# Block queries, keys and values laid out in other runs, part A's output stored by SyncE, nine output-weight pairs loaded inside the first step

## The chip, the cores and the metric

One core of a Trainium2 chip runs the whole program. The metric is the device time of one execution in microseconds. Engines are named as in the profile: PE (TensorE matmuls), PEld (its weight loads), DVE (VectorE), ACT (ScalarE), POOL (GpSimd) and SP (SyncE, which here only issues DMAs). DMAs issued by SP appear on DMA queue q1, those issued by ACT on q10, those issued by POOL on q0. All three share the core's 16 DMA engines.

## The reference, cut to what matters

Two independent parts, joined along the last axis. Part A is a long convolution over 2048 rows of 1024 channels, done by FFT. Part B is a recurrent attention over 64 segments of 32 rows: each segment is led by 8 memory rows that the segment before produced.

```
# part A                                     # part B, for s in range(64):
kv  = shift_conv(k, shift_k) * v             h = concat([mem, x[32*s:32*s+32]])   # 8 + 32 rows
y   = irfft(rfft(kv) * rfft(ssm_k))          q, k, v = h @ Wq, h @ Wk, h @ Wv     # 32 heads of 128
out = q * (y + kv * ssm_D)                   p = softmax(mask(q @ k.T / sqrt(128)))
                                             o = (p @ v) @ Wo
                                             mem = o[:8]; outs.append(o[8:])
```

Only the 8 memory rows and the first 24 rows of `x` of a segment feed the next one. The last 8 rows of each segment, called block rows here, depend on no earlier segment as far as their own queries, keys and values go. 64 x 8 = 512 of them are projected in bulk, ahead of the recurrence.

## The kernel before, in words

The program has two phases. Instructions are issued in the order in which the Python code runs; there is no reordering.

**Part A, 0 to about 407 us.** Four stages, one after another: `stage1` on the filter (scratch `SK1` in DRAM) and, from 70 us, on `kv` (`SU1`); from 176 us the products in the frequency domain, 34 half units that load `Kg` and `Ug` from the scratches and store `SZ`; from 298 us the last stage, 16 rounds `t`. In a round of the last stage `load_z(t + 2)` (L636) issues the loads of `zt` (three buffers, L627) and `qt` (three buffers, L629) on SP, PE makes `y_ps` from `zt` (L642), DVE multiplies it by `qt` into `ot` (two buffers, L645), and POOL stores `ot` to the output (L646). Right after the last round SP issues four `park_w` loads (L676).

Between those instructions, `rows.half(n)` puts in pieces of the bulk projection of the block rows: PE multiplies weights by `hTB` into `ps_q`, `ps_k`, `ps_v` (L173, L176), ACT or DVE empties them. Heads go in four groups `g` of eight. For a group, queries and keys of all 64 segments are gathered in the SBUF tile `stq` (16 KB a partition) and stored to the DRAM tensor `QKBd` by one DMA on ACT's queue (L184). Values are gathered in `stv` 128 rows at a time and stored to `VBd` by four DMAs on POOL's queue, one for each pair of heads `c` (L188). Weights that stay in SBUF are loaded by `res_half` (L112, SP, 256 KB each), the others into a ring of eight (L144). POOL also copies 17 weight pairs from the inputs to DRAM tensors `Wst` (`relay`, L121).

```
183              if m == "k" and j == 7:
184                  nc.scalar.dma_start(QKBd[:, :, g, :].rearrange("s e x -> e s x"),
185                                      self.st[:].rearrange("e s h t r -> e s (h t r)"))
186              if m == "v" and j % 2 == 1:
187                  for c in range(4):
188                      nc.gpsimd.dma_start(VBd[16 * rb:16 * rb + 16, c, g],
189                                          self.sv[:, rb, c * 256:(c + 1) * 256])
```

**Part B's recurrence, about 422 to 2107 us.** A loop over 64 segments `s`, in each of it four groups `g` of heads. For a group, `qk_part` (L748) and `v_part` (L763) project the segment's own rows, `tr_a` transposes and puts the block rows' keys beside them (L785, from `qkb`), `scores` (L807 to L822) and `softmax` follow, `pv` (L848, L850) uses the values and the block values `VB`, and `wo` (L865) adds up the output. After the loop PE makes the output of the block rows (L982).

SBUF does not hold all weights. `resident` pairs stay; 17 pairs of 512 KB, `streamed`, are loaded anew in every step through a ring of five tiles `wring`: `place` (L711) issues the next load on SP, and `done` calls it as soon as PE has used a tile. Each step also loads `qkb` (128 KB of QKBd, SP, L791, issued near the end of the step before, one buffer), `VB` (64 KB of VBd, POOL, L801) and the rows `H` (ACT, L660).

Eleven of the output-weight pairs ("o") are resident. Two are loaded at the end of part A. The memory of the other nine is free only once the bulk projection is over; the loop at L902 issues their 18 halves (L112) on SP, after the first five ring tiles and `qkb`, ahead of the first step:

```
898  for _ in range(RING):
899      place()
900  load_vb(0)
901  qkb = load_b(0)
902  for key in resident:
903      if key[0] == "o" and key not in n_o:
904          for n in range(2):
905              res_half(key, n)
```

Of the kernel before, what the change touches and what calls it, by code (L numbers as in the profile page):

```python
# [9 lines left out]
BF = mybir.dt.bfloat16  # L10
# [11 lines left out]
def fused_kernel(ctx: ExitStack, tc, q, k, v, shift_k, ssm_k, ssm_D, outa, x, mem0, Wq, Wk, Wv, Wo, outb, n_seg):  # L22
# [11 lines left out]
    nc = tc.nc  # L34
# [12 lines left out]
    dram = ctx.enter_context(tc.tile_pool(name="b_dram", bufs=1, space=DRAM))  # L47
    SU1 = dram.tile([128, 32, D], BF, name="SU1")
    SK1 = dram.tile([128, 32, D], BF, name="SK1")
    SZ = dram.tile([128, 32, D], BF, name="SZ")  # L50
    QKBd = dram.tile([n_seg, 128, 4, 128], BF, name="QKBd")
    OLd = dram.tile([n_seg, 128, 256], BF, name="OLd")
    VBd = dram.tile([n_seg, 4, 4, 8, 256], BF, name="VBd")

    pairs = [("qk", g, i) if i < 8 else ("v", g, i - 8) for g in range(4) for i in range(12)]
    pairs[-4:-4] = [("o", 0, i) for i in range(4)]
# [3 lines left out]
    resident = [key for key in pairs if key not in streamed and key not in parked]  # L60
# [65 lines left out]
    class Rows:  # L126
# [27 lines left out]
        def half(self, n, by="A"):  # L154

            for _ in range(n):
                if self.at == 192:
                    return
                iu, j, lo = self.at // 16, self.at % 16 // 2, self.at % 2 * 4
                m, g = units[iu]  # L160
                self.load_to(iu * 8 + 8)
                ws = self.loaded[iu * 8:iu * 8 + 8]
                assert len(ws) == 8
                if lo == 0:
                    self.ps = ps_p.tile([128, 512], F32, tag="pp", name="ps_" + m)
                if m == "q" and self.at % 16 == 0:
                    self.st = stq.tile([128, n_seg, 8, 2, 8], BF, tag="stq", name="stq")
                if m == "v" and self.at % 16 == 0:
                    self.sv = stv.tile([128, 4, 1024], BF, tag="stv", name="stv")
                rb, cs = j // 2, slice(j % 2 * 512, j % 2 * 512 + 512)  # L170
                for kc in range(lo, lo + 4):
                    if m == "v":
                        nc.tensor.matmul(self.ps[:], lhsT=hTB[:, kc, rb * 128:(rb + 1) * 128], rhs=ws[kc][:, cs],  # L173
                                         start=(kc == 0), stop=(kc == 7))
                    else:
                        nc.tensor.matmul(self.ps[:], lhsT=ws[kc][:, j * 128:(j + 1) * 128], rhs=hTB[:, kc, :],  # L176
                                         start=(kc == 0), stop=(kc == 7))
                if lo:
                    if m == "v":
                        self.evac(self.sv[:, rb, cs], self.ps[:], by)  # L180
                    else:
                        self.evac(self.st[:, :, j, int(m == "k"), :], self.ps[:].rearrange("e (s r) -> e s r", r=8), by)
                    if m == "k" and j == 7:
                        nc.scalar.dma_start(QKBd[:, :, g, :].rearrange("s e x -> e s x"),  # L184
                                            self.st[:].rearrange("e s h t r -> e s (h t r)"))
                    if m == "v" and j % 2 == 1:
                        for c in range(4):
                            nc.gpsimd.dma_start(VBd[16 * rb:16 * rb + 16, c, g],  # L188
                                                self.sv[:, rb, c * 256:(c + 1) * 256])
                self.at += 1  # L190
                self.load_to(self.at // 16 * 8 + 8 + self.at % 16 // 2 + 4)

# [5 lines left out]
    def rows_view(ap2d, t):  # L198
        return ap2d.rearrange("(p r) d -> r p d", r=16)[t]
# [415 lines left out]
    with ExitStack() as c3:  # L615
        io = c3.enter_context(tc.tile_pool(name="a3_io", bufs=3, side="right"))
        wk = c3.enter_context(tc.tile_pool(name="a3_wk", bufs=2, side="right"))
        ps_big = c3.enter_context(tc.tile_pool(name="a3_ps", bufs=3, space=PSUM))
        open_res(12)
        rows.load_to(rows.at // 16 * 8 + 16)  # L620
        relay(3)
        zts = {}

        def load_z(t):
            if t < 16:
                zt = io.tile([128, 2, 1024], BF, tag="zt", name="zt")
                nc.sync.dma_start(zt[:], SZ.rearrange("m (h r) d -> r m h d", h=2)[t])  # L627
                qt = wk.tile([128, 1024], BF, tag="qt", name="qt", bufs=3)
                nc.sync.dma_start(qt[:], rows_view(q, t))  # L629
                zts[t] = zt, qt  # L630

        load_z(0)
        load_z(1)
        rows.go(4)
        for t in range(16):
            load_z(t + 2)  # L636
            rows.half(2 + t % 2)
            zt, qt = zts[t]
            pt = ps_big.tile([128, 1024], F32, tag="big", name="y_ps")
            for hf in range(2):  # L640
                for h in range(2):
                    nc.tensor.matmul(pt[:, hf * 512:(hf + 1) * 512], lhsT=G2h[h][:, :],  # L642
                                     rhs=zt[:, h, hf * 512:(hf + 1) * 512], start=(h == 0), stop=(h == 1))
            ot = wk.tile([128, 1024], BF, tag="ot", name="ot")
            nc.vector.tensor_tensor(out=ot[:], in0=pt[:], in1=qt[:], op=ALU.mult)  # L645
            nc.gpsimd.dma_start(rows_view(outa, t), ot[:])  # L646
    ca.close()
    open_res(2)
    act = cw_.enter_context(tc.tile_pool(name="b_act", bufs=1))
# [138 lines left out]

    def load_b(s):
        qkb = act.tile([128, 4, 128], BF, tag="qkb", name="qkb")  # L790
        nc.sync.dma_start(qkb[:], QKBd[s])  # L791
        return qkb

    def new_u(g):
        u = G()
        u.g = g
        u.qkb = qkb[:, g, :]
        return u

    def load_vb(s):  # L800
        nc.gpsimd.dma_start(VB[:], VBd[s].rearrange("c g r x -> (c g r) x"))  # L801

    def scores(u):
        S = ps_ts.tile([128, 4, 40], F32, tag="ts", name="S")
# [94 lines left out]
        place()  # L899
    load_vb(0)  # L900
    qkb = load_b(0)
    for key in resident:  # L902
        if key[0] == "o" and key not in n_o:
            for n in range(2):
                res_half(key, n)
    hT = new_hT()
    h_rows(H, hT, 0)
    for s in range(n_seg):
        us = []
        for g in range(4):  # L910
            if g == 2 and s + 1 == n_seg:
                spare = [key for key in resident if key[0] != "o" and key[1] < 2 and key not in early]
                for key, at in zip([key for key in streamed if key[0] == "o"], spare):
                    nc.sync.dma_start(res[at][:], Wst[key][:])
                    res[key] = res[at]
            u = new_u(g)
            us.append(u)
            qk_part(u, range(0, 4))
            unpark()
            if g >= 1:  # L920
                S = scores(us[g - 1])
            if g >= 2:
                pv(us[g - 2], s, (0, 1))
            if g >= 1:
                softmax(us[g - 1], S)
            qk_part(u, range(4, 6))
            if g >= 2:
                pv(us[g - 2], s, (2, 3))
            qk_part(u, range(6, 8))
            qk_out(u)  # L930
            if g < 3:
                v_part(u, range(0, 8))
                tr_a(u)
                v_out(u)
            unpark()
            if g == 3 and s + 1 == n_seg:
                for s0, s1 in ((0, 32), (32, s)):
                    nc.sync.dma_start(OLs[:, s0:s1].rearrange("e s h r -> e s (h r)"),
                                      OLd[s0:s1].rearrange("s e x -> e s x"))
        Y = ps_acc.tile([128, 512], F32, tag="acc", name="yacc")  # L940
        wo(us[0], Y)
        tr_a(us[3])
        v_part(us[3], range(0, 8), Y)
        v_out(us[3])
        if s + 1 < n_seg:
            H = load_h(s + 1)
        S = scores(us[3])
        if s + 1 < n_seg:
            qkb = load_b(s + 1)
        softmax(us[3], S)  # L950
        pv(us[2], s, (0, 1), "aqaq")
        wo(us[1], Y, range(0, 4))
        pv(us[2], s, (2, 3), "aqaq")
        wo(us[1], Y, range(4, 8))
        wo(us[2], Y)
        pv(us[3], s, (0, 1, 2, 3), "aqta")
        wo(us[3], Y)
        if s + 1 < n_seg:
            hT = new_hT()
            h_rows(H, hT, 8)  # L960
        Y_sb = act.tile([128, 256], BF, tag="PT", name="Y_sb")
        nc.scalar.copy(Y_sb[:], Y[:, 256:512])  # L962
        if s + 1 < n_seg:
            fill_mem(hT, Y_sb)
            idle = ps_acc.tile([128, 512], F32, tag="acc", name="idle")
            keep_warm(idle, 2)
        for dq in range(4):
            nc.gpsimd.dma_start(outb[32 * s:32 * s + 24, dq * 256:(dq + 1) * 256], Y_sb[32 * dq + 8:32 * dq + 32, :])  # L968
        if s + 1 < n_seg:
            load_vb(s + 1)  # L970
# [88 lines left out]
```

## Time and profile before

| | |
|---|---|
| three runs | 2161.88, 2166.8, 2180.03 us (median 2166.8) |
| profiled execution | 2169.6 us, span 2167.7 us, mean granted PE clock 0.959 |
| busy share of the span | PE 82%, PEld 48%, DVE 50%, ACT 39%, POOL 19% |
| DMA | 732.15 MB, mean 338 GB/s |
| q1 (SP) | 683.05 MB, 85.2% of 16 engines' span |
| q0 (POOL), q10 (ACT) | 28.88 MB, 4.2%; 14.62 MB, 2.7% |
| ring loads (L711) | 448 of Wstqk, 320 of Wstv, 315 of Wsto, 512 KB each, 5.9 to 6.4 us to landing |

A share is the part of the span in which an engine was busy, averaged over stages that have different limits. A landing time runs from the issue of a DMA to its completion. In lists of groups the time behind "|" is first the busy time and the mean of one instruction, then the idle time of the engine just ahead of it and what ended most of it.

### The profile page before, as it was taken

The numbers are of one execution on the slowest core, as the hardware profiler recorded it, in microseconds if no ns is written. First come the engines' busy times: TensorE is split into PE (matmuls) and PEld (weight loads), VectorE is DVE, ScalarE is ACT, GpSimd is POOL, SyncE is SP. The second block draws the span as 40 slices with busy tenths as digits, with TensorE's granted clock in tenths as the row PEclk, the third lists the DMA queues.
The fourth block names the chain that finished last, engine by engine and source line by source line (L and its number), as shares of the span: only waits on it lengthen the run. The fifth ranks groups of instructions, "written<-read, shape, count | busy, mean of one in ns | idle before, by whom it ended". The sixth has DMA issues, their size and how long they took to land.

```text
span 2167.7 us, 87967 instructions
## 1 busy us (share of the span) xinstructions
PE 1781.4 (82%) x37808; PEld 1048.6 (48%) x37808; DVE 1091.4 (50%) x3235; ACT 835.5 (39%) x2538; POOL 407.9 (19%) x841
## 2 busy tenths in 40 slices
PE   5777977768888888888888888888888888888889
PEld 2332222345555555555555554555555555555558
DVE  6885842244444445455444455555544545444530
ACT  5445741223334334343334333433333434333320
POOL 4013642201111111111111111111111211111110
PEclk8989998989999999999999999999999999989999
DMA  7798979899999999999999999999999999999990
GB/s 259 271 325 276 364 238 335 256 360 363 363 366 348 356 366 377 346 378 372 357 366 370 351 368 357 376 373 353 373 345 367 364 358 357 358 327 361 351 337 21
DMA packets 275652, 732.15 MB, mean 338 GB/s; under 512 B 65679, under 2 KB 85023, under 8 KB 275261
## 3 DMA queue, kind: packets, MB, share of 16 engines
q1 hardware_dynamic: 214414, 683.05, 85.2%
q0 software_dynamic: 18368, 28.88, 4.2%
q10 hardware_dynamic: 42480, 14.62, 2.7%
q8 instruction: 295, 4.83, 0.9%
q14 instruction: 95, 0.78, 0.1%
HBM read 676.14 MB, written 59.18 MB: 339 GB/s over the span
## 4 chain that ended last, share of the span: by engine, by line
PE 46%; DMA 35%; issue 8%; DVE 5%; ACT 4%; POOL 1%; SPq 0%; ACTq 0%; DVEq 0%; POOLq 0%
DMA wring<-Wstv 16%; PE qkacc L748 13%; DMA wring<-Wstqk 9%; PE yacc L865 9%; PE vacc L763 4%; PE otacc L848 3%; PE yacc L763 3%; PE pl L982 3%; PE tp L777 2%; DMA wring<-Wsto 2%; DMA H<-in_B_x_dram 2%; PE ps_v L173 1%; PE ps_k L176 1%; PE otacc L850 1%; PE ps_q L176 1%
## 5 line engine op out<-in xcount | busy, mean ns | idle before, releaser
L748 PE MATMUL qkacc<-Wqk,hT 128*32 128x512 bf16 x4096 | 351.0, 383 | 3.7 <-issue 3.7
L853 ACT CAST OT<-otacc 128x80 bf16<-128x80 f32 x1024 | 183.3, 234 | 391.5 <-PE otacc L850 385.5
L856 POOL COPY OL<-OT 128x64 bf16<-128x64 bf16 x252 | 64.6, 257 | 1328.6 <-ACT OT L853 1328.6
L763 PEld LDWEIGHTS <-hT 128*32 128x32 bf16 x8192 | 213.4, 97 | 174.5 <-issue 107.3
L865 PE MATMUL yacc<-Wo,OT 128*32 128x256 bf16 x5632 | 258.5, 287 | 24.3 <-issue 20.1
L748 PEld LDWEIGHTS <-hT 128*32 128x32 bf16 x8192 | 177.3, 96 | 207.2 <-issue 59.4
L865 PEld LDWEIGHTS <-OT 128*32 128x32 bf16 x8192 | 216.9, 100 | 91.4 <-issue 54.8
L748 PE MATMUL qkacc<-wring,hT 128*32 128x512 bf16 x2048 | 205.9, 388 | 20.7 <-DMA wring<-Wstqk 19.2
L848 PE MATMUL otacc<-PT,vsb 32*128 32x64 bf16 x2048 | 147.3, 193 | 58.9 <-ACT OT L853 48.9
L763 PE MATMUL vacc<-wring,hT 128*32 128x256 bf16 x2560 | 117.2, 276 | 79.2 <-DMA wring<-Wstv 78.1
L786 DVE COPY QT<-tp 128x256 bf16<-128x256 bf16 x256 | 74.7, 292 | 198.4 <-PE tp L777 192.2
L717 ACT COPY wring<-park 128x1024 bf16<-128x1024 bf16 x128 | 129.9, 1015 | 114.5 <-PE qkacc L748 110.0
L748 PE MATMUL qkacc<-Wearly,hT 128*32 128x512 bf16 x2048 | 164.6, 395 | 8.3 <-DVE hT L891 4.3
L821 DVE TENSOR_REDUCE mx<-S 128x4 f32<-128x160 f32 x256 | 83.1, 325 | 170.5 <-PE S L818 167.5
L754 ACT CAST qks<-qkacc 128x512 bf16<-128x512 f32 x256 | 150.5, 588 | 40.6 <-PE qkacc L748 36.9
L832 DVE TENSOR_REDUCE sm<-P 128x4 f32<-128x256 bf16 x256 | 107.6, 420 | 102.9 <-ACT P L830 102.9
L763 PE MATMUL vacc<-Wv,hT 128*32 128x256 bf16 x3584 | 157.7, 274 | 0.3 <-issue 0.2
L865 PE MATMUL yacc<-wring,OT 128*32 128x256 bf16 x2520 | 140.0, 287 | 17.4 <-issue 15.8
L850 PE MATMUL otacc<-PT,VB 32*128 32x64 bf16 x2048 | 143.5, 190 | 8.9 <-issue 7.2
L883 DVE COPY hT<-x_tp 128x192 bf16<-128x192 bf16 (+1 forms) x64 | 23.0, 359 | 236.5 <-PE x_tp L882 236.5
L968 POOL DMA_DIRECT2D out_dram<-Y_sb x256 | 129.7, 513 | 37.7 <-ACT Y_sb L962 34.7
L848 PEld LDWEIGHTS <-vsb 32*128 32x128 bf16 x2048 | 84.5, 93 | 105.5 <-issue 95.9
(220 smaller groups left out, 2926.6 us busy)
## 6 DMA issues: line engine op xcount, KB each, us to landing
wring<-Wstqk SPq DMA_DIRECT2D x448, 512.0 KB, 6.4
wring<-Wstv SPq DMA_DIRECT2D x320, 512.0 KB, 5.9
wring<-Wsto SPq DMA_DIRECT2D x315, 512.0 KB, 6.1
SK<-s_sb SPq DMA_DIRECT2D x8, 1024.0 KB, 6.6
SU<-s_sb SPq DMA_DIRECT2D x8, 1024.0 KB, 7.3
QKBd<-stq ACTq DMA_DIRECT2D x4, 2048.0 KB, 20.5
Kg<-SK SPq DMA_DIRECT2D x16, 512.0 KB, 8.1
Ug<-SU SPq DMA_DIRECT2D x16, 512.0 KB, 8.4
```

Source lines behind the costliest of these rows:

```text
L717: nc.scalar.copy(t[:, 0, :], park[key][0][:])
L748: nc.tensor.matmul(u.qk[p0:p0 + 32, :], lhsT=hT[:, kc, :], rhs=w[t][:, c2 * 512:(c2 + 1) * 512], start=(kc == 0), stop=(kc == 7), tile_pos ...
L754: nc.scalar.copy(u.qks[:], u.qk[:])
L763: nc.tensor.matmul(u.vacc[32 * c:32 * c + 32, 0:256], lhsT=hT[:, kc, :], rhs=w[kc % 2][:, c * 256:(c + 1) * 256], start=(kc == 0 and Y is ...
L786: nc.vector.tensor_copy(u.QT[:].rearrange("e (c j) r -> e c j r", c=2), tv[:, 0])
L821: nc.vector.tensor_reduce(out=mx[:], in_=S[:], op=ALU.max, axis=AX.X)
L832: nc.vector.tensor_reduce(out=sm[:], in_=P[:], op=ALU.add, axis=AX.X)
L848: nc.tensor.matmul(o, lhsT=u.v[r, i * 128:(i + 1) * 128], rhs=PTv[r, i, 0], start=True, stop=False, tile_position=(32 * c, 0))
L850: nc.tensor.matmul(o, lhsT=VB[r, i * 128:(i + 1) * 128], rhs=PTv[r, i, 1], start=False, stop=True, tile_position=(32 * c, 0))
L853: nc.scalar.copy(u.OT[:, 2 * c:2 * c + 2, :], ov[:, :, 0:40])
L865: nc.tensor.matmul(Y[32 * dq:32 * dq + 32, 256:512], lhsT=u.OT[:, hh, 0:32], rhs=w[hh % 2][:, dq * 256:(dq + 1) * 256], start=(u.g == 0 an ...
L968: nc.gpsimd.dma_start(outb[32 * s:32 * s + 24, dq * 256:(dq + 1) * 256], Y_sb[32 * dq + 8:32 * dq + 32, :])
```

## The change

Four edits. `QKBd` is laid out by group: a store writes whole runs of 16 KB per partition, and the load of a segment gathers four pieces of 256 B per partition (before: 1 KB in one piece). `VBd` is laid out by pair of heads, group, segment: one store takes all four pairs of 128 rows, and a load takes 16 runs of 4 KB (before: 64 KB in one run). Part A's output is stored by SP instead of POOL. The 18 halves of the nine output-weight pairs are issued six at a time, ahead of groups 0, 1 and 2 of the first step. The tiles, the arithmetic and the order of the instructions of PE, DVE and ACT are as before.

```
-    QKBd = dram.tile([n_seg, 128, 4, 128], BF, name="QKBd")
+    QKBd = dram.tile([4, 128, n_seg * 128], BF, name="QKBd")
...
-    VBd = dram.tile([n_seg, 4, 4, 8, 256], BF, name="VBd")
+    VBd = dram.tile([4, 4, n_seg, 8, 256], BF, name="VBd")
...
                     if m == "k" and j == 7:
-                        nc.scalar.dma_start(QKBd[:, :, g, :].rearrange("s e x -> e s x"),
-                                            self.st[:].rearrange("e s h t r -> e s (h t r)"))
+                        nc.scalar.dma_start(QKBd[g], self.st[:].rearrange("e s h t r -> e (s h t r)"))
                     if m == "v" and j % 2 == 1:
-                        for c in range(4):
-                            nc.gpsimd.dma_start(VBd[16 * rb:16 * rb + 16, c, g],
-                                                self.sv[:, rb, c * 256:(c + 1) * 256])
+                        nc.gpsimd.dma_start(VBd[:, g, 16 * rb:16 * rb + 16].rearrange("c s r x -> (s r) c x"),
+                                            self.sv[:, rb, :].rearrange("p (c x) -> p c x", c=4))
...
             nc.vector.tensor_tensor(out=ot[:], in0=pt[:], in1=qt[:], op=ALU.mult)
-            nc.gpsimd.dma_start(rows_view(outa, t), ot[:])
+            nc.sync.dma_start(rows_view(outa, t), ot[:])
...
     def load_b(s):
         qkb = act.tile([128, 4, 128], BF, tag="qkb", name="qkb")
-        nc.sync.dma_start(qkb[:], QKBd[s])
+        nc.sync.dma_start(qkb[:], QKBd[:, :, s * 128:(s + 1) * 128].rearrange("g e x -> e g x"))
...
     def load_vb(s):
-        nc.gpsimd.dma_start(VB[:], VBd[s].rearrange("c g r x -> (c g r) x"))
+        nc.gpsimd.dma_start(VB[:], VBd[:, :, s].rearrange("c g r x -> (c g) r x"))
...
     load_vb(0)
     qkb = load_b(0)
-    for key in resident:
-        if key[0] == "o" and key not in n_o:
-            for n in range(2):
-                res_half(key, n)
+    n_o = [key for key in resident if key[0] == "o" and key not in n_o]
...
     for s in range(n_seg):
         for g in range(4):
...
+            for key in (n_o[3 * g:3 * g + 3] if s == 0 else ()):
+                for n in range(2):
+                    res_half(key, n)
             u = new_u(g)
```

## The prediction

> **What bounds the kernel now.** I read the windows by stage first, then the DMA view of single stretches, then the queue's own waits, then the time line around each stall. The windows put the loop over the 64 segments (467 to 2043 us) beside four stretches ahead of it. Columns: PE, PEld, DVE, ACT, POOL busy, granted clock, DMA share, GB/s.
>
> ```profile
> 70.00:176.00 106.00, 86.20 (x370) 36.78 (x367) 88.26 (x129) 52.08 (x71) 8.44 (x16) 0.94 0.81 273
> 176.00:216.00 40.00, 28.52 (x152) 8.70 (x152) 26.92 (x45) 22.12 (x41) 21.07 (x23) 0.91 0.99 306
> 318.00:356.00 38.00, 23.69 (x99) 9.97 (x98) 8.57 (x7) 5.28 (x9) 9.80 (x19) 0.81 0.94 285
> 422.00:431.00 9.00, 5.66 (x122) 2.96 (x126) 2.65 (x8) 2.88 (x4) 1.65 (x3) 1.00 0.63 215
> 467.00:2043.00 1576.00, 1329.81 (x33396) 815.52 (x33400) 791.72 (x2677) 609.67 (x2123) 252.47 (x607) 0.97 0.98 361
> ```
>
> In the loop the 16 DMA engines are busy 98% of the time and PE 84%: the weight tiles streamed into the ring set the step, so DMA time added to a step lengthens it. Ahead of the loop the rate falls to 285 to 306 GB/s while the engines stay 94 to 99% busy: they move something inefficient. The DMA view of 185 to 215 us names it (packets, MB, share):
>
> ```profile
> q1 hardware_dynamic: 2941, 5.56, 51.8%
> q10 hardware_dynamic: 8208, 2.10, 33.0%
> ```
>
> That is one QKBd store on ACT's queue: 2 MB in 8192 packets of 256 B, 33.0% x 16 x 30 us / 8208 = 19.3 ns each. It takes 158 engine-us, 9.9 us of all 16 engines. The page gives the two transfers of this tensor (KB each, median us to landing):
>
> ```profile
> qkb<-QKBd SPq DMA_DIRECT2D x64, 128.0 KB, 6.1
> QKBd<-stq ACTq DMA_DIRECT2D x4, 2048.0 KB, 20.5
> ```
>
> SP waits for that landing: in the program's list of waits the DMAs of SP and ACT take eight completion semaphores in turn, and the eighth DMA after a store waits for it. The queue's own waits (total, times, longest), and PE's stalls in the time line:
>
> ```profile
> SPq L627 <- DMA QKBd<-stq: 18.4, 1, 18.4
> ...
> SPq L112 <- DMA QKBd<-stq: 11.4, 1, 11.4
> SPq L519 <- DMA QKBd<-stq: 9.6, 1, 9.6
> ...
> SPq L112 <- DMA VBd<-stv: 7.3, 1, 7.3
> ```
>
> ```profile
> 216.68 0.64 PE L547 MATMUL Kre_ps<-Kg,Mre 128*64 128x512 bf16 x2 [4.17 <-DMA Kg<-SK]
> ...
> 352.47 1.89 PE L642 MATMUL y_ps<-zt,G2h 128*128 128x512 bf16 x4 [12.08 <-DMA zt<-SZ]
> ...
> 446.52 0.62 PE L763 MATMUL vacc<-wring,hT 128*32 128x256 bf16 x8 [15.03 <-DMA wring<-Wstv]
> ```
>
> The first two stalls follow stores 2 and 3; the last is the first step, where SP has 18 output-weight halves (4.7 MB) ahead of the ring's next tile, and none of them starts before the last VBd store has landed.
>
> **The change, part by part.** The order of PE, DVE and ACT stays the same; POOL loses 16 part A stores and 48 VBd stores, SP gains the 16, and 12 of the 18 halves move behind ring loads.
>
> *QKBd stores as whole runs (4).* Runs of 16 KB replace 8192 pieces. The trace has no such store; the nearest are the 4 KB packets, 174 ns on average in the packet records of the loop, so 2 MB is 512 x 174 = 89 engine-us, 5.6 us of all engines, against 9.9. Bounds: 5.1 (4 KB at the median of 159 ns) and 9.9 (no gain). I take 5.6 and a landing near 8 us. What that is worth, store by store:
> Store 1 (110.9 us): SP stands still until 131.4, an SU store takes 11.2 us, weights issued at 135.7 reach PE at 145.3. PE's last product of the stage starts at 172.1, though DVE ended its input at 166.9, having lost 3.7 us itself to PE. PE cannot pass DVE: at most 3.7 + 5.2 less a normal lag of 1.2 = 7.7. I take 6.5 (3 to 7.7).
> Store 2 (193.1): the stall of 4.2 goes; the half units then run at their cadence of 3.1 us on PE. 4 (0 to 4.2).
> Store 3 (324.8): PE loses 12.1, but the stretch to 386 is held by DMA, so I count DMA time: 4.3 us of packets, and about 4 us in which the engines ran dry while SP was held (342 to 351). 8.5 (3 to 13).
> Store 4 (407.1): SP waits until 420.7 for PE to free ring memory, so this DMA time is spare. 0.
> Sum 19 us (6 to 25).
>
> *Part A's stores on SP.* Sixteen issues of 0.55 us leave POOL, where they hide behind nothing that is late. On SP each waits for DVE's ot (1.22 us each), and behind it queue zt and qt of three rounds later and a weight half. qt already waits for ot(t), since it has three buffers; zt waits for PE's product of the same round, 1.2 us earlier. From an issue, zt needs 7.6 us, y_ps 1.0, ot 1.2: 10 us for three rounds, 3.4 a round, against some 3.7 now, which DMA sets at 396 GB/s. So nothing inside the stage, if the store lands in the 5.7 us it takes now; if it lands like qt behind the loads of its own queue (7.3), two rounds take 0.3 + 7.3 + 1.2 = 8.8 us, 0.7 a round longer, 11 us in all. At the end, park_w was issued at 384.5 ahead of the last ot; it now comes behind it (385.7), and PE already waits 3.4 us for it: +2. I take +2 (0 to +13).
>
> *VBd stores 128 rows at once.* 64 stores of 0.53 us of POOL become 16 with four times the rows each. Bounds for one: 0.53 to 2.1 us; POOL has room either way. In DRAM the pieces stay 512 B. The last one goes out near 422 instead of 425.5, where POOL had also stood 3.2 us, so the Wo halves start some 3 us earlier. The VB load (64 KB, 4.8 us) keeps pieces of 512 B per partition and is used in a later group: 0.
>
> *Wo inside the first step.* The bytes are the same. Six halves instead of 18 stand ahead of the next ring tile, which is issued near 430 instead of 440.5; PE gains about 10 us there, but 3.1 MB (8.5 us) then compete with the ring in the rest of the step. As the loop is held by DMA from the next step on, what stays is the DMA time that no longer runs dry: 0.37 x 9 us = 3.3 in 422 to 431. I take 3.5, with the VBd edit (0 to 10).
>
> *The load of a block, 64 times.* Now 128 packets of 1 KB, 47 ns each in the packet records, 6.0 engine-us. After it, each partition gathers four pieces of 256 B: 512 pieces. The trace has no 256 B read. Its bounds: a quarter of the 1 KB packet, 11.8 ns (no loss), and the piece of 512 B in the OLd load at the end, 2 KB packets of four pieces at 117 ns, 29 ns. The 256 B store piece, 19.3 ns, is nearest. The pieces of a partition lie 128 x 8192 x 2 bytes apart, 2 MiB. 512 x 19.3 = 9.9; (9.9 - 6.0) / 16 = 0.24 us a step, 15.6 us over 64, times 0.98: 15. Where pieces share the engines with other queues they overlap (the shares add up to more than 100% in parts of the stores), so I take 13 (0 to 36). Its latency has cover: issued at 1002.8, first used at 1011.1; 8.3 us against 6.1.
>
> The Trainium skill, "DMA: Bandwidth & Descriptors", section "Latency and other measured facts", speaks against this edit: a row pitch of 2 MiB cuts copies to 164 GB/s from 207 at 512 KiB, and that is the pitch here. By its ratio the piece would cost 24 ns, an estimate from that page, the loss 25 us and the whole change +4.5. No run here has that pitch; it is weighed below.
>
> *Sum.* -19 + 2 - 3.5 + 13 = -7.5 us against the profiled execution: 2169.6, of which the span is 2167.7. Its time is 2.8 above the median of the runs, 2166.8. A run after: 2166.8 - 7 = 2160.
>
> **The rivals.** *The load is free in the loop.* For it: overlapping packets, and 2% of 26 us of DMA idle, in which 0.24 us would fit. Against: the idle is in crumbs, and PE waits 106 times for a Wstv tile alone (78 us). With part A's gain at 24 and the first step's at 3.5: 2166.8 - 27.5 = 2139; with the upper ends of both, 2132.
>
> *The pieces of one load hinder one another,* as they all lie at power-of-two distances and 16 engines read them at once. For it: a gathered 512 B piece (64 KB pitch) takes 29 ns, a single one (H) 27. Against: zt, in 2 KB runs at 32 KB pitch, takes 88 ns a run, as plain runs do. Halfway between 19.3 and 29, 24 ns: (12.3 - 6.0) / 16 x 64 = 25 us, 12 over the forecast's 13: 2172. The rule cited above is of this kind; no trace agrees with it yet.
>
> *The load is dear.* A piece read alone costs well over a piece stored; SP's queue is served in order, so the ring tile behind each of the 64 loads is late by it. At 29 ns: (14.9 - 6.0) / 16 x 64 = 36 us, 2182. At 40 ns, twice the row: 58 us, 2204. It decides from 32 ns on, where the loss passes 42 us and the total 2189. Against: 512 B pieces already cost 29.
>
> *SP's order takes part A's gain back.* The store lands in 7.3 us behind its own queue's loads, +11, and store 3 then gives nothing: 2160 + 11 + 8.5 = 2179.5.
>
> *The 16 KB runs are no faster than the pieces:* the stores keep 20 us, all of the 19 goes, 2179.
>
> **How the numbers follow.** Forecast 2160 at 0.34, own range 2146 to 2176; the free load 0.32; hindered pieces 0.09; the dear load 0.17; SP's order 0.05; no faster stores 0.03. About 1%, 22 us, is what a measurement of this kernel can tell. Faster by more: the free load and a little of the forecast, 0.35. Slower by more: the dear load and some of the last two, 0.19. Within: 0.46. Range 2132 (all upper gains, no loss) to 2190 (a piece at 32 ns).
>
> **What would show it.** Right: no QKBd wait on SP over 3 us, stores landing under 10 us, part A some 18 us shorter (the loop's second step starting near 446 instead of 467), the 15 us stall at L763 under 6, and the loop some 13 us longer, with qkb landing near 7 us and a DMA share still at 0.98. Wrong: a loop that is not longer, one longer by over 30 us, or DVE's wait for out_dram growing past 27 us.

## The result, and the profile after

The changed kernel takes 2161.4 us (median of 13 runs, 2146.3 to 2170.0) against 2170.0 for the kernel before in the same session (13 runs, 2161.9 to 2180.0): ratio 0.995, 95% interval 0.9929 to 0.9971. A second session gave 2158.4 against 2175.2, 0.9928 (0.9898 to 0.9958). Both lie within the 1% named as no change, 9 to 17 us on the faster side; the prediction was 2160, 7 us faster. The profiled execution of after took 2148.3 us (span 2146.4), 13 us less than its own median, so its absolute times flatter the change; I read differences between landmarks, not its span.

The windows of after, over the stretches that answer to those shown of before (same columns: PE, PEld, DVE, ACT, POOL busy, granted clock, DMA share, GB/s). Line numbers of after are two lower from the middle of the file on.

```profile
70.00:168.00 98.00, 83.15 (x363) 36.35 (x369) 88.26 (x129) 52.54 (x71) 3.07 (x4) 0.98 0.83 296
168.00:208.00 40.00, 31.55 (x167) 9.91 (x171) 27.28 (x46) 24.36 (x45) 20.04 (x20) 0.91 1.01 361
304.00:342.00 38.00, 31.29 (x129) 13.04 (x129) 10.45 (x9) 7.04 (x12) 3.08 (x4) 0.91 0.99 357
404.00:412.00 8.00, 4.46 (x84) 2.28 (x84) 1.38 (x4) 2.88 (x4) 1.30 (x2) 1.00 0.71 238
448.00:2024.00 1576.00, 1324.81 (x33419) 809.97 (x33409) 791.59 (x2678) 609.66 (x2125) 249.92 (x604) 0.98 0.99 361
```

The first stretch holds the same DVE work (88.26 us) in 98 us that took 106. In the second and third, the DMA engines are a little busier than before (1.01 and 0.99 against 0.99 and 0.94; a share above 1 comes of packets whose times overlap) and move 361 and 357 GB/s in place of 306 and 285. The fourth, the first step, still has its engines only 71% busy. The DVE, ACT and POOL work of the loop is the same.

The DMA view of 180 to 200 us around store 2 of `QKBd` (packets, MB, share of 16 engines), and the two transfers of this tensor from the DMA view of the whole execution (KB each, median us to landing):

```profile
q1 hardware_dynamic: 2480, 4.67, 69.5%
q10 hardware_dynamic: 144, 2.10, 25.2%
```

```profile
QKBd<-stq ACTq DMA_DIRECT2D x4, 2048.0 KB, 10.9
...
qkb<-QKBd SPq DMA_DIRECT2D x64, 128.0 KB, 6.2
```

The store is now 128 packets of 16 KB (and 16 small ones): 25.2% x 16 x 20 us = 81 engine-us, 5.0 us of all engines in place of 9.9. It lands in 10.9 us where it took 20.5 (medians of 10.2 to 12.0 in all ten traces of the new layout, 16.7 to 20.5 in the four of the old); the load lands in 6.2 where it took 6.1.

SP's own waits, from the list of after in its order (total, times, longest), and PE's stalls in the time line:

```profile
SPq L709 <- PE qkacc L746: 366.3, 370, 4.0
SPq L709 <- DMA wring<-Wstqk: 291.2, 297, 3.7
...
SPq L112 <- DMA VBd<-stv: 7.4, 1, 7.4
...
SPq L644 <- DMA QKBd<-stq: 5.7, 1, 5.7
...
SPq L112 <- DMA QKBd<-stq: 3.4, 1, 3.4
```

```profile
323.04 1.89 PE L640 MATMUL y_ps<-zt,G2h 128*128 128x512 bf16 x4 [5.33 <-DMA zt<-SZ]
...
372.03 1.03 PE L683 MATMUL park_t<-ident,park_w 128*128 128x128 bf16 x8 [6.02 <-DMA park_w<-in_B_Wv_dram]
...
420.59 0.62 PE L761 MATMUL vacc<-wring,hT 128*32 128x256 bf16 x8 [6.56 <-DMA wring<-Wstv]
...
429.01 0.40 PE L761 MATMUL vacc<-wring,hT 128*32 128x256 bf16 x8 [2.61 <-DMA wring<-Wstv]
...
436.89 0.40 PE L863 MATMUL yacc<-wring,OT 128*32 128x256 bf16 x8 [2.37 <-DMA wring<-Wsto]
```

Of 39.4 us in which SP stood for a `QKBd` store, 9.1 are left. The stall after store 2 is gone, that of 12.1 after store 3 has become 5.3, and the 15.0 of the first step 6.6, 2.6 and 2.4. What is left after store 3 is not SP's wait: the `zt` tile that PE stands for there was issued at 310.8, 0.2 us behind the store, and took 12.2 us to land, where the median is 6.9. The wait for park_w grew from 3.4 to 6.0, and the VBd wait stayed. The first two lines bear on the loop: SP stands longest not for transfers but for PE's products at L746, which hand back the ring tile that the next load needs. It was so before the change:

```profile
SPq L711 <- PE qkacc L748: 383.9, 375, 4.0
SPq L711 <- DMA wring<-Wstqk: 260.1, 299, 3.3
```

Landmarks of the time line, us (first Kg load: start of part A's second stage; first zt load: of its last; third ring load: end of part A; H load of the second and the last segment: the loop):

```
                     Kg     zt     ot first..last  3rd ring   H 2nd   H last
before              176.0  307.5   315.5..384.4     420.7     459.1   2069.2
after               167.9  293.8   301.8..363.6     402.4     440.3   2048.6
after, 2nd session  175.0  300.5   309.6..370.9     410.3     448.3   2049.0
```

### The profile page after: what moved, and what is told of

It is laid out like the page before. It is cut to its first block, busy times and chain, and to the rows that moved or that the text cites. A ratio compares the mean times of both kernels' runs of the same rounds, so it can differ in the third digit from the quotient of the medians.

```text
span 2146.4 us, 87846 instructions
## 1 busy us (share of the span) xinstructions
PE 1770.8 (83%) x37779; PEld 1041.6 (49%) x37808; DVE 1091.0 (51%) x3235; ACT 836.3 (39%) x2538; POOL 377.1 (18%) x777
## 4 chain that ended last, share of the span: by engine, by line
PE 47%; DMA 34%; DVE 8%; issue 6%; ACT 5%; POOL 0%; SPq 0%; ACTq 0%; DVEq 0%; POOLq 0%
DMA wring<-Wstqk 13%; PE qkacc L746 12%; DMA wring<-Wstv 12%; PE yacc L863 9%; DMA wring<-Wsto 4%; PE otacc L846 3%; PE vacc L761 3%; PE yacc L761 3%; PE pl L980 3%; PE tp L775 3%; DMA out_dram<-ot 2%; PE ps_k L176 1%; PE ps_v L173 1%; PE otacc L848 1%; DVE S L820 1%
## 5 line engine op out<-in xcount | busy, mean ns | idle before, releaser
L746 PE MATMUL qkacc<-Wqk,hT 128*32 128x512 bf16 x4096 | 350.4, 383 | 3.2 <-issue 3.2
L854 POOL COPY OL<-OT 128x64 bf16<-128x64 bf16 x252 | 64.6, 256 | 1331.7 <-ACT OT L851 1331.7
L746 PEld LDWEIGHTS <-hT 128*32 128x32 bf16 x8192 | 178.3, 96 | 213.2 <-issue 69.8
L863 PE MATMUL yacc<-Wo,OT 128*32 128x256 bf16 x5632 | 252.8, 282 | 27.1 <-issue 22.7
L863 PEld LDWEIGHTS <-OT 128*32 128x32 bf16 x8192 | 212.2, 98 | 96.7 <-issue 63.5
L746 PE MATMUL qkacc<-wring,hT 128*32 128x512 bf16 x2048 | 206.9, 390 | 28.0 <-DMA wring<-Wstqk 26.1
L746 PE MATMUL qkacc<-Wearly,hT 128*32 128x512 bf16 x2048 | 165.3, 398 | 6.9 <-DVE hT L889 3.6
L863 PE MATMUL yacc<-wring,OT 128*32 128x256 bf16 x2520 | 135.3, 280 | 23.0 <-issue 16.1
## 6 DMA issues: line engine op xcount, KB each, us to landing
QKBd<-stq ACTq DMA_DIRECT2D x4, 2048.0 KB, 10.9
```

The costliest lines, as they stand in the source:

```text
L746: nc.tensor.matmul(u.qk[p0:p0 + 32, :], lhsT=hT[:, kc, :], rhs=w[t][:, c2 * 512:(c2 + 1) * 512], start=(kc == 0), stop=(kc == 7), tile_pos ...
L863: nc.tensor.matmul(Y[32 * dq:32 * dq + 32, 256:512], lhsT=u.OT[:, hh, 0:32], rhs=w[hh % 2][:, dq * 256:(dq + 1) * 256], start=(u.g == 0 an ...
```

## The experiments

Every ratio is to the kernel before on the same chip. Its interval is about 0.3% to either side, 6.5 us, so a difference between two kernels is good to about 9 us; where less is read, it is from landmarks in the traces.

Theory, from the prediction: `QKBd`'s stores give part A about 19 us and its gathered loads take 13 back in the loop, with little from the rest. Rivals: the load is free; the load is dear; the gain comes from the other edits.

### The changed kernel once more

> The changed kernel once more, for a second profile and as a base for the others. The prediction's theory (part A and the first step give some 20 us, the gathered load takes some 13 us back in the loop): 0.995 of before, near 2160 us, and in a profile at before's granted clock (0.96) the loop from the second step's qkb issue to the last one near 1620 us against 1610 before. The rival (the load is free, and the first profile's loop of 1608 us is the rule): a loop within 3 us of before whatever the clock, so a time near 2148.

2158.4 us, 0.9928 (0.9898 to 0.9958): the reference for the three that follow, which ran beside it. The loop in its trace, 1600.7 us at a clock of 0.964, is neither the 1620 of the theory nor within 3 us of before's 1610. One execution does not settle it: in the eight traces with the gathered load once a step the loop takes 1600.7 to 1628.3 us (median 1612), and the two loops without a load, which are one program, read 1594.9 and 1601.3.

### QKBd's edit undone

```
-    QKBd = dram.tile([4, 128, n_seg * 128], BF, name="QKBd")
+    QKBd = dram.tile([n_seg, 128, 4, 128], BF, name="QKBd")
...
-                        nc.scalar.dma_start(QKBd[g], self.st[:].rearrange("e s h t r -> e (s h t r)"))
+                        nc.scalar.dma_start(QKBd[:, :, g, :].rearrange("s e x -> e s x"),
+                                            self.st[:].rearrange("e s h t r -> e s (h t r)"))
...
-        nc.sync.dma_start(qkb[:], QKBd[:, :, s * 128:(s + 1) * 128].rearrange("g e x -> e g x"))
+        nc.sync.dma_start(qkb[:], QKBd[s])
```

> The changed kernel with QKBd in its old layout (256 B pieces stored, 1 KB pieces loaded), the other three edits kept. Prediction's theory: the other edits alone give about 1.5 us, so within 4 us of before, ratio 0.998 to 1.001; part A long again (ring loads at L709 near 420 us instead of 402), loop 13 us shorter than with the gathered load. Rival (load free): 18 us over the changed kernel, that is 8 to 10 us slower than before or equal to it with something else lost in the loop.

2174.9 us, 1.0021 (0.9992 to 1.005): nothing is left of the gain. It is 16.5 us over the changed kernel, near the 18 that the rival of a free load named; its loop, 1610.0 us, is not the 13 us shorter than the loops with the gathered load that the theory had. SP's list has the store's waits again:

```profile
SPq L645 <- DMA QKBd<-stq: 12.0, 1, 12.0
SPq L518 <- DMA QKBd<-stq: 11.1, 1, 11.1
...
SPq L112 <- DMA QKBd<-stq: 10.5, 1, 10.5
```

The other three edits together are worth nothing that can be measured.

### The load taken out of the loop, in either layout

The same edit in the new layout and in the old one:

```
-        if s + 1 < n_seg:
-            qkb = load_b(s + 1)
```

> The changed kernel without the 63 loads of qkb inside the loop: every segment uses segment 0's block queries and keys. Beside the changed kernel this prices the gathered load. Prediction's theory: 9.3 engine-us a load (512 pieces at 18.1 ns) is 0.57 us of all 16 engines, so 36 us shorter than the changed kernel if the loop is held by DMA alone, 2125 us. Rival (load hidden): less than 10 us shorter.

> QKBd in its old layout and no load of qkb in the loop (segment 0's block queries and keys for all), the other edits kept. Beside undo_qkbd this prices the load in 1 KB pieces: 6.0 engine-us, 0.38 us, 24 us in all by the prediction's theory; near 0 by the rival. Beside noload_gather, whose loop is the same, it gives part A's share of the layout alone: 19 us by the prediction, some 18 by the two profiles.

With the gathered layout 2146.4 us, 0.9871 (0.9839 to 0.9904); with the whole one 2166.0, 0.997 (0.9941 to 0.9999). Two differences follow. Between the two, without any load in the loop, lies what the stores alone are worth: 19.6 us. Against the kernels with the load, a gathered load costs 2158.4 - 2146.4 = 12.0 us over the loop and a whole one 2174.9 - 2166.0 = 9.0. The gather's surplus is 3 us, where its DMA time is 13; but 3 is a difference of differences, uncertain by some 13.

Neither load's DMA time comes back in full when the load is gone: a gathered one's 9.3 engine-us (512 records of 18.1 ns) are 0.58 us of all engines, 36.6 us over 63 loads, of which 12 came back; of 23.6 for the whole ones, 9 came back, each uncertain by some 9. The window of the loop without the gathered load, and SP's first wait, show how little room there is:

```profile
448.00:2024.00 1576.00, 1330.23 (x33628) 818.44 (x33624) 795.65 (x2688) 614.66 (x2139) 256.08 (x616) 0.98 0.97 359
```

```profile
SPq L709 <- PE qkacc L746: 386.0, 370, 4.0
```

With no load of it at all, DMA still reads 0.97 (0.99 with it) and the rate does not rise. SP's wait for PE at L746 is 386 us here (366 with the loads). I read from this that the loop is not set by DMA alone: its queue waits on PE for free ring tiles and PE waits on it for full ones.

### The load five times

To enlarge the surplus, the load is issued five times a step, four times into tiles that nothing reads; the ring gives up one of its five tiles for the space. A twin does the same in the old layout.

```
-    RING = 5
+    RING = 4
...
             qkb = load_b(s + 1)
+            for i in range(4):
+                xq = xp.tile([128, 4, 128], BF, tag=f"xq{i}", name=f"xq{i}")
+                nc.sync.dma_start(xq[:], QKBd[:, :, (s + 1) * 128:(s + 2) * 128].rearrange("g e x -> e g x"))
```

> The changed kernel, with each step's load of block queries/keys (a 256 B gather) issued five times, the four extra ones into tiles of their own that nothing reads, and the weight ring cut from five tiles to four to make room. It is read against its twin with whole 1 KB pieces. By the packet records a gathered load takes 9.3 engine-us against 6.0 for a whole one, 0.2 us of all engines. Theory 1 (this DMA time is paid in full in a loop that DMA sets): five loads cost 5 x 13 = 65 us more than the twin's five, less 19.6 us of part A's gain, so this kernel is some 45 us slower than the twin. Theory 2 (only about 3 us per load and 64 steps is paid, as the pair without loads has it): 15 - 19.6, so some 5 us faster than the twin. A difference between -5 and 45 is the size of the term itself: (difference + 19.6) / 5 for one load over the 64 steps.

> The twin: block queries/keys in the layout of before (the other three edits kept), each step's load issued five times in whole 1 KB pieces, and a ring of four tiles. Four extra loads of 0.375 us of DMA time are 94 us if paid in full, so some 2260 to 2280 us with what the shorter ring costs. Theory 1: about 45 us faster than the gathered twin. Theory 2: about 5 us slower than it.

Gathered 2505.8 us, 1.1517 (1.1486 to 1.1549); whole 2485.2, 1.1413 (1.138 to 1.1447). The gathered one is 20.6 us slower, between the two theories: (20.6 + 19.6) / 5 = 8 us for one load over the loop, uncertain by some 3, if the fifth load costs what the first does. The windows of the two loops give it again without part A, gathered first:

```profile
447.50:2392.70 1945.20, 1506.05 (x34120) 856.87 (x34106) 807.73 (x2728) 621.69 (x2171) 256.05 (x620) 0.90 0.94 315
```

```profile
466.30:2383.80 1917.50, 1483.76 (x34116) 852.05 (x34100) 807.78 (x2728) 621.54 (x2171) 255.76 (x620) 0.92 0.92 320
```

1945.2 - 1917.5 = 27.7, 5.5 a load, from one execution of each. The packet records have 20.0 ns for a gathered piece here and 48.1 for a whole one: (512 x 20.0 - 128 x 48.1) / 16 = 0.26 us a load, 80 us for 63 steps of five, of which 28 to 40 were paid. In what form is open: PE is busy 22 us longer in the gathered loop for the same products, at a granted clock of 0.90 against 0.92, and these runs do not tell whether the loads hold PE up by the wait for ring tiles, by the lower clock, or by both. Among the six runs of either kernel the time shows no clear fall with the clock.

My 2260 to 2280 us for the twin was a miss: four more whole loads and a ring of four tiles cost (1.1413 - 1.0021) x 2175 = 303 us over the kernel with one load and five. No kernel had the short ring alone, so how this splits is open. The share of DMA falls to 0.92 and the rate to 320 GB/s, so it is not a lack of DMA bandwidth.

### The three other edits undone, one at a time

Part A's store by POOL again (`nc.gpsimd` for `nc.sync`, one word):

> The changed kernel with one part undone: part A's sixteen stores are issued by GpSimd again. Theory (each of the three smaller edits is worth a few us at most): 2 us faster than the changed kernel, ratio to before near 0.993; PE's wait for park_w back from 6.0 to about 3.4 us, the last ot still near 62 us behind the first. Rival (SP's order costs part A more than its trace shows): 7 us faster or more, ratio 0.990 or less, with the stretch from the first to the last ot some 5 us shorter.

2159.2 us, 0.9946 (0.9922 to 0.997), not to be told from the changed kernel. In the trace the end of part A has its 3 us back:

```profile
369.99 0.62 PE L683 MATMUL park_t<-ident,park_w 128*128 128x128 bf16 x8 [3.26 <-DMA park_w<-in_B_Wv_dram]
```

From the first ot to the third ring load it takes 97.6 us, against 100.6 to 101.4 in the seven traces of the new layout with SP's store. First to last ot, 62.7, is not shorter than after's 61.8: SP's order costs nothing inside the stage.

VBd in four stores of 32 rows, as before:

> The changed kernel with one part undone: block values stored in four stores of 32 rows each in place of one of 128. Theory (the VBd store hides behind nothing that waits for it, and the first output weights still start 9.4 us after the third ring load): no change, ratio near 0.994 to 0.995, the gap from the third ring load to the first output-weight half within 1 us of 9.4. Rival (the prediction's: the last store leaves 3 us earlier and the halves with it): 3 us slower, ratio 0.996, the gap 12 us.

2162.7 us, 0.994 (0.9914 to 0.9966): no change. The first half of Wo leaves 8.5 us behind the third ring load (after: 9.4).

All eighteen Wo halves ahead of the first step:

> The changed kernel with one part undone: all eighteen output-weight halves ahead of the first step's ring tiles again. Theory (bytes are the same, and DMA sets the loop): the first step's stall on the ring goes from 6.6 back to about 15 us, the second step starts 8 us later, and the loop behind it is about as much shorter, so the whole is 0 to 3 us slower, ratio 0.994 to 0.996. Rival (the stall is on the path to its full length): 8 us slower, ratio 0.998.

2159.3 us, 0.9957 (0.9926 to 0.9987). The stall is back:

```profile
436.36 0.62 PE L761 MATMUL vacc<-wring,hT 128*32 128x256 bf16 x8 [15.09 <-DMA wring<-Wstv]
```

yet the second H load comes 39.2 us behind the third ring load, and 37.9 in after (38.4 in before), where my expectation had 8 us between them. Other traces with after's first step have 37.6 to 40.5, so moving 12 halves into the step gains nothing that can be told from this spread. Part of the reason is in after's time line: three waits for ring tiles, 6.6, 2.6 and 2.4 us, stand in place of one of 15.

### Wo one group later

```
-            for key in (n_o[3 * g:3 * g + 3] if s == 0 else ()):
+            for key in (n_o[3 * g - 3:3 * g] if s == 0 and g else ()):
```

> The changed kernel, with the first step's output-weight halves issued before groups 1, 2 and 3 in place of 0, 1 and 2, so that the first step's ring tiles stand ahead of all of them. Theory (bytes set the loop): the stall of 6.6 us on the ring nearly goes, and later waits take most of its place; 0 to 3 us faster than the changed kernel, ratio 0.992 to 0.994. Rival (the stall is on the path): 6 us faster, ratio 0.991 or less. Second rival (the halves come too late for the first step's output): slower by the wait for them, above 0.996.

2156.4 us, 0.9924 (0.9895 to 0.9953). The second H load comes 31.1 us behind the third ring load, 6.8 sooner than in after. Whether the loop gives this back is not shown: from there to the last H load it takes 1612.2 us against 1608.3, well within the spread of single executions, and the runs do not tell the two kernels apart.

### The last two: a combination, and QKBd's edit alone

> The changed kernel with part A's stores on GpSimd again and the first step's output-weight halves issued before groups 1, 2 and 3. Theory (both are small gains that add): from the traces, 4 us at the end of part A (last ot to third ring load 35 in place of 39 us) and up to 7 us in the first step, of which the loop gives back 4: some 6 us faster than the changed kernel, ratio 0.990 to 0.992. Rival (what is won ahead of the loop is given back in it, since the bytes are the same): as the changed kernel, 0.993 to 0.995.

> The kernel before with the one edit of the block queries/keys. Theory (this edit is the whole of the gain, the other three sum to nothing): ratio 0.992 to 0.995, all four stores landing in 11 us, and part A shorter by some 20 us. Rival (the other edits carry part of it, the first step's above all): 0.997 or more.

Part A's store on POOL with Wo one group later: 2152.3 us, 0.9898 (0.9872 to 0.9923). The kernel before with the `QKBd` edit and nothing else: 2150.9, 0.99 (0.9858 to 0.9941). Both are better by their medians than the whole change. Against its second session (0.9898 to 0.9958) the intervals overlap; against its first (0.9929 to 0.9971) that of the combination does not. By its own expectation the combination speaks for the theory that the two small gains add (0.990 to 0.992) and against the rival that the loop takes them back (0.993 to 0.995). Its trace agrees ahead of the loop: the second H load comes 30.1 us behind the third ring load, and the third ring load 32.7 behind the last ot, against 37.9 and 38.8 in after. The last H loads, 2049.9 and 2050.1 against 2048.6, decide nothing here, since after's profiled execution was 13 us faster than its median and these two are at theirs.

The `QKBd` edit alone made the kernel 13 to 31 us faster. The prediction's terms for it, -19 + 13 = -6, lie outside; with 19.6 us for the stores, these runs leave at most some 7 us for the load's surplus, and speak for less.

## Why the prediction was right, step by step

**What bounds the kernel.** Right for the stretches ahead of the loop. For the loop, "DMA time added to a step lengthens it" held for a third to a half of that time only, by the loads taken out (12 of 36.6, 9 of 23.6) and by the five loads (28 to 40 of 80).

**QKBd stores, -19.** Right in sum: 19.6 us between the two kernels without loads, uncertain by some 9, and the stages add up to the same. By stage, with the landmarks of all ten traces of the new layout beside the four of the old: to the first Kg load 170 against 176.6 in the median, so 6.5 as predicted (167.9 to 175.0 in single executions; counted from the issue of store 1 itself, 56.1 to 60.6 us against 64.6 to 66.7); the second stage 125.6 against 131.7, 6 where 4 was predicted, with 4.2 as its bound; from the first zt to the third ring load 113.2 in before against 106.3 with this edit alone, 7 where 8.5 was. The packet time was near (5.0 us a store, taken at 5.6), the landing not: 10.9 us, taken at 8. Two waits of SP went past the 3 us named as a limit, and beside store 3 PE still stood 5.3 us for a `zt` tile.

**Part A's stores on SP, +2.** Right by the trace: 2.3 us in the old layout (107.5 with SP's store and the other two edits, 105.2 in before, first ot to third ring load) and about 3 in the new, for the reason given, park_w behind the last ot; too little for the runs by itself. DVE's wait for out_dram did grow past 27 us, to 36.3, which I had named as a sign of being wrong. It was a poor sign: with POOL's store the wait is 28.7 and the stage as long, so the growth fell into time that DVE had.

**VBd and Wo in the first step, -3.5.** The failed step. "The last one goes out near 422 instead of 425.5 ... so the Wo halves start some 3 us earlier": it does go out 3 us earlier against the ring (1.7 us behind the third ring load in place of 4.8), but 7.0 us then pass from its end of issue to the first half, where 4.1 passed before. The halves start 9.4 us behind that load in both. Nor is the earlier store the VBd edit's doing: with four stores again the last one goes out 1.9 us behind the ring load, without the 3.2 us that POOL stood in before, and 6.0 us pass. Why more time passes when the store leaves sooner is open. The stall that the Wo edit was to shorten went to later ring tiles of the same step, so that the second H load comes 37.9 us behind the third ring load in after and 38.4 in before. The two edits came to nothing that can be measured.

**The load, +13.** Too large: 3 us by the pair without loads, uncertain by 13, and 8 by the five loads, which alone show its sign. The piece was well priced (18.1 ns in after, 19.3 assumed), so the mis-sized factor is the last one, "times 0.98": a busy share of 0.98 was read as the part of added DMA time that lengthens the step. The trace of before already held the reading against it, SP's 383.9 us of waits for PE on the ring. The loop of the profiled execution was 1.8 us shorter, not longer, which was one of the signs of being wrong; the one of the second session was 9.4 us shorter. Single executions spread too far to show this term, and only the five loads show it by itself.

**The sum.** -19.6 + 2.5 + 0 + 3 to 8 is -14 to -9; the runs have -9 and -17. That the forecast of -7 came out close is in part luck, since two errors stood against each other: the load priced 5 to 10 us too high, the first step credited with 3.5 us that did not come.

**The rivals.** The free load was the nearest of them and cannot be put aside by the plain kernels: the edit alone, the edit undone and the loops in the traces lean its way. The five loads speak against it, if the fifth costs what the first does. The dear load and the hindered pieces are out: 36 and 25 us of surplus were at stake, and a piece took 18.1 ns with 2 MiB between the four pieces of a partition. The Trainium skill's page "DMA: Bandwidth & Descriptors", section "Latency and other measured facts", gives its rates by the row pitch from one partition to the next. That pitch is 16 KiB in the new layout (8192 values of 2 bytes). The prediction put the rule to the 2 MiB between a partition's own pieces, of which the page does not speak, so its 24 ns was an estimate by likeness alone, and no run here tests the page's figures. SP's order took nothing back in part A, and the runs of 16 KB are twice as fast as the pieces.

## What to carry to other kernels

When a scattered layout must be paid either in the store or in the load, look at which of them something stands in line behind: here 2 MB stores of 256 B pieces held SP's queue three times, for 10 to 18 us, while 64 gathers of the same pieces lay beside other transfers. A DMA share of 0.98 does not say that DMA sets the time: read whether the queue waits for transfers or for the engine that frees its tiles, and count added DMA time at a part of itself where it waits for both. A stall that goes is worth what the next landmark gains: here the first step's wait of 15 us was split into three shorter ones, and the second step came half a microsecond sooner.

## What the runs showed of the hardware

- By the packet records of before and after, a 16 KB packet of a `QKBd` store takes 628 ns, 26 GB/s on one engine; a 256 B piece 18.1 ns read and 19.2 stored, 13 to 14 GB/s; 1 KB read takes 47 ns, 22 GB/s.
- Four extra loads of 128 KB per step, 0.375 us of DMA time each, with one ring tile less, cost 4.8 us a step. Which of the two did it was not tried.
- The time of one and the same kernel goes along with the granted clock: over 66 runs of the kernel before, clock 0.952 to 0.970, the time falls by 13 us for each 0.01 of clock (correlation -0.74). In a loop that DMA set alone it should hardly do so; but a run with more stalls also shows a lower clock (in before's stall after store 3, 342 to 351 us, PE did nothing and the clock read 0.55), and the runs cannot tell cause from effect.
